# Rows 4 and 5 of a 2-D transform taken from rows 2 and 1, turned in DRAM

## The chip, the cores and the metric

The kernel runs on one core of one Trainium2 chip. The metric is device time in microseconds (us); each kernel is run several times, next to runs of the kernel before on the same chip. Engines: TensorE (PE in the profile; its sequencer PEq), VectorE (DVE), ScalarE (ACT; its DMA queue ACTq), GpSimd (POOL), SyncE (SP; its DMA queue SPq). A profiled run gives a page of summaries and a trace. The record calls a run slow when it is over 1.5% above the fastest of its kernel, and fast otherwise; where slow runs are among those quoted, I say so. "Granted clock" is the share of its full clock that TensorE was given.

## The reference

Four batches, eight heads, 768 tokens of 64 channels. Attention with a band of 96 and 8 global tokens, then a real 2-D Fourier transform over 768 tokens and 512 channels, a normalisation, and a feed-forward product of 512 x 2048 x 512.

```python
def _moe_ref(x, w_ch1, w_ch2) -> np.ndarray:           # x: (4, 768, 512), out of the attention
    X = np.fft.fft(x, axis=1)
    X = np.fft.fft(X, axis=2)
    mixed = np.real(X).astype(np.float32)
    u = x + mixed
    mu = np.mean(u, axis=-1, keepdims=True)
    var = np.mean((u - mu) ** 2, axis=-1, keepdims=True)
    un = (u - mu) / np.sqrt(var + 1e-06)
    ch = np.maximum(un @ w_ch1, 0.0) @ w_ch2
    return (u + ch).astype(np.float32)
```

## The kernel before

Tokens of a batch are handled as six "rows": row r holds the tokens 6m + r, m on the 128 partitions. The attention output x goes to DRAM (`xd`) and comes back in that form (`xr`). The transform over tokens gives y (matmuls `py`), the one over channels gives u (matmuls `pu`, 16 for two rows). Two rows make a chunk, and a chunk goes through normalise, transpose (`ptu` to `unT`, from batch 2 on by DMA), `ph` and `pg`, the two feed-forward products. A y with its columns backwards, kept for a second use, is a mirror copy. A static plan in Python orders the work of each engine once, at build time.

Other names in the lines below: `qs` and `vs` are loaded q, k and v, `pt` the transposes of q and k (into `qkT`), `sc` the attention scores, `er` their exponentials, `zy` a y copied out of PSUM, `hT` a `ph` copied out, `ob` a finished row. A fill matmul is one whose result nobody uses. PSUM is the memory in which the results of matmuls lie; the kernel uses it in pieces called banks.

```python
PAIRS = ((1, 2), (0, 3), (4, 5))                       # rows of the three chunks of a batch
...
def rd():                                              # x comes back by rows
    XR[b] = buf("xr", b, [P, NS, Dm], FP16, 3)
    for c in ((0, 3), (3, 6)):
        eng.dma_start(XR[b][:, c[0]:c[1]], XD[b].rearrange("(m r) d -> m r d", r=6)[:, c[0]:c[1]])
...
def ysrc(rs, rd):                                      # where a y comes from: direct, or a mirrored copy
    if (rs, rd) in POS:
        return rs, rd, False
    return (6 - rs) % 6, (4 - rd) % 4, True
...
# u_unit: one pu group of 16 matmuls for each of the three chunks
for (a, rd), (r2, d2, mir) in src.items():
    yy = Y[(b, r2, d2, "r") if mir else (b, r2, d2)]
    o = pu[:, a, rd * P:(rd + 1) * P]
    for x in range(2):
        nc.tensor.matmul(o, yy[:, x, :], t2_sb[:, rd, (0 if x == 0 else (2 if mir else 1)), :],
                         start=(x == 0), stop=(x == 1))
...
# the result of a row goes out in one DMA
(nc.scalar if c < 6 else nc.sync).dma_start(out[b].rearrange("(m r) d -> m r d", r=6)[:, rs, :], cell[0])
```

The softmax here doesn't subtract the row's maximum and nothing guards it: scores larger than these inputs give would overflow.

## Time and profile before

| | before |
|---|---|
| time, median of 3 | 272.46 us (272.37 to 273.26) |
| profiled span | 270.1 us, granted TensorE clock 1.000 |
| real matmul work in 10 us (columns / 2400, fill left out), 50 to 260 us | 8.7 to 10.1 us |
| DMA moved | 41.25 MB |

The page gives busy time by engine and the chain of work that ended last. The lines that carry the reading stand in the prediction below.

### The profile page before, as it was taken

What the parts mean: (1) busy time and instruction counts of PE and PEld (TensorE: products, weight loads), DVE (VectorE), ACT (ScalarE), POOL (GpSimd) and SP (SyncE); (2) the same over time, 40 slices, a digit from 0 to 9 for tenths busy, and PEclk for the clock granted to TensorE, in tenths of its full rate; (3) what the DMA queues carried; (4) which work ended last, traced back from release to release, by engine and by line L of the source; (5) the groups of instructions that cost most, each with busy time, mean ns of one, the idle gap of its engine ahead of it and who ended that gap; (6) DMA issues with size and microseconds to landing.
All of it is one profiled execution on the core that took longest, in us unless ns stands there. A gap on an engine that the chain in (4) does not pass through costs nothing.

```text
span 270.1 us, 6015 instructions
## 1 busy us (share of the span) xinstructions
PE 257.7 (95%) x2425; PEld 174.3 (65%) x2425; DVE 177.0 (66%) x357; ACT 136.9 (51%) x234; POOL 72.5 (27%) x125
## 2 busy tenths in 40 slices
PE   7789899999999999999999999999989999999994
PEld 3345587787775456767887655687676666767443
DVE  4576938767699999975799777789964424211112
ACT  2877437778631327868344557882464252515000
POOL 1582708549214572363001320120000010100000
PEclk9999999999999999999999999999999999999999
DMA  7999979999999998998059982024602221210122
GB/s 209 292 274 311 205 228 213 206 200 205 201 231 293 287 271 209 219 174 137 0 149 245 143 197 61 0 43 110 203 0 44 95 62 55 62 41 38 40 80 78
DMA packets 82447, 41.25 MB, mean 153 GB/s; under 512 B 45812, under 2 KB 78068, under 8 KB 82292
## 3 DMA queue, kind: packets, MB, share of 16 engines
q1 hardware_dynamic: 70804, 28.81, 48.8%
q0 software_dynamic: 4224, 4.19, 9.7%
q10 hardware_dynamic: 7392, 7.87, 9.7%
q8 instruction: 19, 0.31, 0.5%
q14 instruction: 8, 0.07, 0.1%
HBM read 32.47 MB, written 9.44 MB: 155 GB/s over the span
## 4 chain that ended last, share of the span: by engine, by line
PE 79%; DVE 11%; SPq 3%; DMA 2%; issue 1%; POOL 1%; ACT 1%; DVEq 0%; POOLq 0%
PE ph L1103 32%; PE pg L1126 24%; PE pu L990 4%; PE sc L569 4%; PE pav L698 3%; DVE x L718 2%; PE pt L531 2%; DMA qs<-in_q_dram 2%; PE py L901 2%; SPq L405 2%; PE pg L1155 1%; PE py L905 1%; PE ptu L1072 1%; PE pav L687 1%; PE py L908 1%
## 5 line engine op out<-in xcount | busy, mean ns | idle before, releaser
L1103 PE MATMUL ph<-unT,w 128*128 128x256 f16 x768 | 94.9, 273 | 0.0
L1126 PE MATMUL pg<-w,hT 128*128 128x512 f16 x368 | 86.0, 379 | 0.0
L1103 PEld LDWEIGHTS <-w 128*128 128x128 f16 x768 | 71.8, 98 | 15.9 <-issue 4.4
L1109 ACT ACTIVATE hT<-ph 128x512 f16<-128x512 f32 x59 | 35.1, 597 | 54.0 <-PE ph L1103 52.2
L1126 PEld LDWEIGHTS <-hT 128*128 128x128 f16 x368 | 35.1, 98 | 35.7 <-issue 1.1
L592 ACT ACTIVATE er<-sc 128x992 f16<-128x992 f32 (+2 forms) x42 | 38.0, 924 | 19.6 <-DMA qs<-in_q_dram 7.2
L1137 DVE SCALAR_TENSOR_TENSOR ob<-pg,sm,u 128x512 f32<-128x512 f32 x23 | 17.2, 748 | 44.4 <-PE pg L1126 33.8
L1110 DVE TENSOR_SCALAR hT<-ph 128x512 f16<-128x512 f32 x37 | 25.4, 688 | 14.4 <-PE ph L1103 14.1
L423 POOL CAST qk<-qs 128x768 f16<-128x768 f32 x25 | 22.6, 908 | 44.7 <-DMA qkT<-qk 18.8
L607 DVE TENSOR_TENSOR ex<-er,mk 128x992 f16<-128x992 f16 (+2 forms) x42 | 27.6, 672 | 3.5 <-ACT er L592 3.4
L1047 POOL TENSOR_SCALAR sm<-sm 128x2 f32<-128x2 f32 x12 | 2.8, 233 | 74.6 <-ACT un L1040 74.2
L1011 DVE SCALAR_TENSOR_TENSOR u<-pu,xr 128x512 f32<-128x512 f32 x24 | 15.7, 686 | 6.3 <-PE pu L990 6.2
L718 DVE TENSOR_TENSOR x<-pav,rc 128x512 f16<-128x512 f32 (+1 forms) x27 | 17.1, 632 | 1.2 <-DVE rc L717 0.3
L569 PE MATMUL sc<-qkT 64*128 64x256 f16 (+1 forms) x192 | 16.4, 261 | 0.6 <-ACT v L470 0.4
L1040 ACT ACTIVATE un<-un 128x512 f16<-128x512 f16 x24 | 14.9, 622 | 3.3 <-DMA unT<-un 2.9
L698 PEld LDWEIGHTS <-ex 128*128 128x128 f16 x352 | 15.0, 97 | 2.0 <-DVE rc L717 0.4
L698 PE MATMUL pav<-v,ex 128*128 128x65 f16 x352 | 16.1, 193 | 0.0
L922 ACT ACTIVATE zy<-py 128x512 f16<-128x512 f32 x16 | 9.2, 593 | 12.8 <-DVE eA L855 8.0
L569 PEld LDWEIGHTS <-qkT 64*128 64x128 f16 x192 | 6.3, 94 | 12.0 <-issue 9.3
L479 POOL CAST v<-vs 128x768 f16<-128x768 f32 x12 | 11.8, 980 | 7.6 <-DMA vs<-in_v_dram 7.5
L330 PE MATMUL fill<-eg 128*128 128x512 f16 x45 | 12.4, 424 | 1.4 <-DVE eg L1188 1.2
L540 DVE COPY qkT<-pt 128x1536 f16<-128x1536 f16 x12 | 11.4, 952 | 1.1 <-PE pt L531 1.0
(109 smaller groups left out, 288.5 us busy)
## 6 DMA issues: line engine op xcount, KB each, us to landing
vs<-in_v_dram SPq DMA_DIRECT2D x24, 192.0 KB, 6.9
w<-in_moe_w_ch_dram POOLq DMA_DIRECT2D x8, 512.0 KB, 9.7
qs<-in_q_dram SPq DMA_DIRECT2D x9, 384.0 KB, 6.8
qs<-in_k_dram SPq DMA_DIRECT2D x9, 384.0 KB, 7.3
out_dram<-ob ACTq DMA_DIRECT2D x12, 256.0 KB, 3.4
out_dram<-ob SPq DMA_DIRECT2D x11, 256.0 KB, 2.0
xd<-x ACTq DMA_DIRECT2D x12, 192.0 KB, 3.3
xr<-xd ACTq DMA_DIRECT2D x6, 384.0 KB, 3.9
```

Of the source, the lines that this page charges most:

```text
L423: nc.gpsimd.tensor_copy(d, s)
L569: nc.tensor.matmul(pa[:, s, c0:c0 + cw], TT[n][lo:lo + 64, 1, i * P:(i + 1) * P], TT[n][lo:lo + 64, 0, i * P:i * P + cw], start=(not inps) ...
L592: A(mine(), cut(pa), AF.Exp, 0.0, 0.125)
L607: VT(o, mine(), m, op=ALU.mult)
L698: nc.tensor.matmul(po[:, jj, hh * 65:(hh + 1) * 65], lhsT, v16[b % 2][:, i, h, 0:65], start=(jp == 0 and a == 0), stop=(a == len(ops) - 1) ...
L718: VT(X[b][:, 2 * jp:2 * jp + 2, first * Dh:(first + nh) * Dh].rearrange("p j (h d) -> p j h d", d=Dh), pv[:, :, :, 0:Dh], rc.to_broadcast( ...
L1011: V.scalar_tensor_tensor(u[:, a].rearrange("p (n r) -> p n r", r=4), pu[:, a].rearrange("p (r n) -> p n r", r=4), 1.0, XR[b][:, (r0, r1)[a ...
L1103: nc.tensor.matmul(ph[:, a * CH:(a + 1) * CH], w1[:, d, jb * P:(jb + 1) * P], UNT[c][:, d, :], start=(d == 0), stop=(d == ND - 1))
L1109: pl.later([("ACT", act(512), lambda: A(dst, ph, AF.Relu)), ("DVE", dve(512), lambda: V.tensor_scalar_max(dst, ph, 0.0))], [], e, [("h", c ...
L1110: ("DVE", dve(512), lambda: V.tensor_scalar_max(dst, ph, 0.0))],
L1126: nc.tensor.matmul(pg, HT[c][:, jb, t * P:(t + 1) * P], w2[:, jb, :], start=(jb == 0), stop=(jb == NJ - 1))
L1137: V.scalar_tensor_tensor(cell[0], pg, MV[c][:, t, 3:4], UT[c][:, t, :], op0=ALU.mult, op1=ALU.add)
```

## The change

The transform of a real x has a symmetry: row 6 - r is row r with columns and tokens backwards. So rows 5 and 4 need no `pu` of their own, if x is added in turned form and the result is turned back. Columns can be read backwards on chip; tokens lie on partitions and are turned in DRAM, x once (`xe`) and each result row once (`oe`). A second part is for batch 0: three tokens are summed on VectorE first, so that 16 `py` matmuls vanish, and the first chunk is put ahead of later work.

```diff
+            rows = XD[b].rearrange("(m r) d -> m r d", r=6)
 ...
+            XE[0] = dr.tile([2, P, Dm], FP16, tag="xe", name=f"xe_{b}", bufs=2)
+            eng.dma_start(XR[b][0], rows[:, 1:3])
+            eng.dma_start(XE[0], rows[::-1, 4:6].rearrange("m a d -> a m d"))      # turned in DRAM
+            eng.dma_start(XR[b][2], rows[:, 0:4:3])
 ...
+        pl.later([(on, 0.5, lambda: eng.dma_start(XR[b][1][:, :, 0:Dm], XE[0].rearrange("a p d -> p a d")))], [("xr", b)], 0.0,
 ...
-    PAIRS = ((1, 2), (0, 3), (4, 5))
+    PAIRS = ((1, 2), (5, 4), (0, 3))
 ...
+                if pr == 1:                                     # u of rows 5 and 4 from the pu of rows 1 and 2
+                    o, xx = u[:, a, 1:Dm + 1], xr[:, 1 - a, 1:Dm + 1]
+                    i = pu[:, a].rearrange("p (r n) -> p r n", r=4)[:, ::-1, ::-1].rearrange("p r n -> p n r")
 ...
+        def g3():                                               # batch 0: sums of three before py, on VectorE
 ...
+            def back():                                         # second hop of a turned result
+                o = out[b].rearrange("(m r) d -> m r d", r=6)[::-1, rs, :]
+                eng.dma_start(o.rearrange("m (h d) -> h m d", h=2), cell[1].rearrange("m (h d) -> h m d", h=2))
```

(Cut: the mirror copies that go, edge columns, the order of units, four casts, those of two head pairs, moved to ScalarE, constants of the plan.)

## The prediction

> **What bounds the kernel now.** I read the page first, then the chain of waits in order of time, then the timeline by engine around the places where that chain changes owner. From the page, the engine shares, the chain's shares and the two costliest groups:
>
> ```profile
> PE 257.7 (95%) x2425; PEld 174.3 (65%) x2425; DVE 177.0 (66%) x357; ACT 136.9 (51%) x234; POOL 72.5 (27%) x125
> ...
> PE 79%; DVE 11%; SPq 3%; DMA 2%; issue 1%; POOL 1%; ACT 1%; DVEq 0%; POOLq 0%
> ...
> L1103 PE MATMUL ph<-unT,w 128*128 128x256 f16 x768 | 94.9, 273 | 0.0
> L1126 PE MATMUL pg<-w,hT 128*128 128x512 f16 x368 | 86.0, 379 | 0.0
> ```
>
> TensorE carries 79% of the chain that ends last, two thirds of it in the two feed-forward products (ph and pg). Busy 95% is not proof of full use, so I counted columns: matmul columns divided by 2400 per us. From 0 to 46 us real work fills about two thirds of the time (the rest is waiting and fill matmuls); from 50 us to 260 us every stretch of 10 us holds 9.1 to 10.5 us of it. So there are two regimes: a start limited by a chain of dependences, and after 46 us a TensorE that is simply full. The chain of waits shows the border:
>
> ```profile
> 34.07 5.44 PE py L901 x48
> 39.51 0.89 PE pu L990 x16
> ...
> 45.17 0.89 PE pu L990 x16
> 46.06 0.87 PE ph L1103 x8
> ...
> 49.01 0.87 PE ph L1103 x8
> ```
>
> 48 py matmuls take 5.44 us (0.113 each), 16 pu matmuls 0.89 us, and the first ph starts at 46.06 us. After that TensorE idles visibly only three times, 1.66 us in all. The timeline (start, duration; in brackets idle before it and what ended it):
>
> ```profile
> 85.28 0.29 PE L687 MATMUL pav<-vG,eg 128*128 128x260 f16 x1 [0.26 <-DVE x L718]
> 103.27 0.27 PE L905 MATMUL py<-t,eA 128*128 128x256 f16 x1 [0.50 <-DVE zy L924]
> 201.18 1.05 PE L990 MATMUL pu<-t,zy 128*128 128x128 f16 x16 [0.90 <-ACT zy L922]
> ```
>
> The DMA queue of SyncE matters for what follows. Its issues, and the GpSimd cast that waits for the last of them:
>
> ```profile
> 34.84 0.81 SPq L745 DMA_DIRECT2D xr<-xd  x2
> ...
> 42.50 2.81 SPq L371 DMA_DIRECT2D vs<-in_v_dram  x2
> 45.42 2.94 SPq L405 DMA_DIRECT2D qs<-in_k_dram  x1
> 53.98 0.83 POOL L423 CAST qk<-qs 128x768 f16<-128x768 f32 x1 [0.27 <-DMA qs<-in_k_dram]
> ```
>
> A load issued at 45.42 us landed at 53.95 us: 8.5 us later. By the landing times in the trace the vs loads ahead of it (issued from 42.50) landed at 51.4 and 52.3 us. The queue is backlogged all the way from 36 to 54 us.
>
> **What the Trainium skill says.** (1) "DMA: Bandwidth & Descriptors", section Queues, rings and completion order: SyncE owns one ring on each of 16 DMA engines, and each consumes descriptors in ring order. The trace agrees: landings from this queue come in the order of issue, 1 to 2 us apart, at 42.5, 44.1, 44.9, 45.6, 50.1, 51.4, 52.3, 53.9 us. (2) Same page, Latency and other measured facts: two of the engines are usually slower. The trace agrees that the last engine sets a landing: the load landing at 42.5 us had half of its engines done by 40.2. (3) "TensorE: Matmul & The Clock Gate", section Back-to-back issue gap: N/2.4 + 2.5 ns warm, which is 56 and 109 ns for 128 and 256 columns; the trace has 0.89/16 = 55.6 ns and 0.113 us. (4) "Perfetto Trace Analysis", Sequencer Loop: an instruction waits for its semaphore in its engine's queue. Each engine's order is fixed when the kernel is built, so one late operand holds everything behind it.
>
> **The change part by part.**
> - Rows 4 and 5 of the transform reuse the product of rows 2 and 1: four groups of 16 pu matmuls vanish, 4 x 0.89 = 3.56 us of TensorE. In batch 0, rows 0 and 3 are summed on VectorE first: 16 of 60 py matmuls vanish, 16 x 0.113 = 1.81 us. The built order confirms both: 2425 matmuls become 2346 (one more is a fill). **Sum 5.4 us**, nearly all on the full engine.
> - 16 mirror copies vanish (12 on ScalarE 7.1 us, 2 on VectorE 0.6, 2 on GpSimd 1.2). Beside other work, but they end the 0.90 us idle at 201 us.
> - Added on VectorE: six sums in batch 0 (before the py evictions; 2 x 0.42 + 4 x 0.28 = 2.0 us by the rows of equal shape) and edge-column copies (8 x 0.17 = 1.3 us over the kernel). Both hidden, in my judgement: the py in front of them runs to 38.2 us, and the sums should end near 37.4.
> - Added on DMA: per batch 256 KB turned in DRAM and read back, and two stores turned through DRAM. Late in the kernel the DMA share is low (0.14 to 0.4 in the rows by stretch after 160 us), so nothing there; the last chunk is not turned.
> - First chunk's chain: with 8 fewer py before it pu starts about 0.6 us earlier (then limited by the y evictions), ends near 39.75; add, normalise, transpose, copy follow without the mirror copies on ScalarE and without pu 2 and 3 on TensorE. 39.75 + 0.95 (add of a row with its sum, to the end of sm) + ScalarE free at 41.3, normalise 0.65, transpose 0.3, two copies of 0.42 and waits: the first ph near **43.3 instead of 46.06**.
>
> If that were all: 5.4 us of work less, about 0.6 us more idle at the start, up to 1.7 us of gaps gone: 272.5 - 5.4 + 0.6 - 1 = about 266.7.
>
> **The new wait.** The built order shows what stands behind it. VectorE: two copies of the first chunk's transpose, then a copy of an edge column of the turned tokens (xr1), add of rows 5 and 4, and only then the eviction of the first and second ph. ScalarE: normalise of that second chunk before it evicts the third ph. TensorE: ph, ph, one qk transpose, then a third ph that waits for VectorE's first eviction, since ph has two buffers. On SyncE the read of xr1 is issued after both vs loads of the second head pair, exactly the slot before the 45.42 issue. By ring order it lands after 52.3 us; with 256 KB where the next load had 384 KB (landed 53.9), I estimate **53.2 us**. Then VectorE needs 0.15 (column) + 1.5 (two adds, timed at 0.69 + 0.08 each) + 0.35 (column, mean) + 0.7 (eviction) = 2.7: third ph near 55.9. TensorE was out of work at 43.3 + 1.75 + 0.8 = 45.9. **A stall of 10 us.**
>
> The sum, from the third ph on: before, 270.1 - 49.0 = 221.1 us remained. After, add ptu 0.45 and pu 0.89 not done yet, take 3 x 0.89 for batches 1 to 3: 219.8; less about 1 us of gaps: 218.8. End 55.9 + 218.8 = 274.7 us of span; timed runs are 2.0 to 2.4 us above the span, so about **276.8**, and I say 276.5 because the chain of batch 1 gets its data ready during the stall.
>
> **The rivals.**
> 1. xr1 lands early, because fewer descriptors stand ahead than I think or the queue drains faster: the stall shrinks to 0 to 4 us and the time is 266.5 to 271. For: its issue needs only the turned rows, in DRAM by about 40 us, and 46 us would be enough. Against: landing order equals issue order in every case I looked at.
> 2. The stall is there but is repaid: batch 1 loses its later waits on VectorE, 97% busy from 80 to 110 us. At most the 1.66 us of gaps plus the start of batch 1: 273 to 276.
> 3. Worse: ScalarE now casts two head pairs of batch 2, issues the turned reads, and waits for each store to land before turning it (3.4 us to landing in the row of stores from ScalarE). It is 51% busy, but waits in order delay the exponentials; 1 to 3 us more: 278 to 280.
> 4. TensorE work does not matter at all, hidden behind VectorE: against it, real work of 10 us in nearly every 10 us after 50.
>
> **Range and chances.** I give the long stall 75 to 80%, centred at 276.5 with about 2 us either way; a small one or none the rest, spread from 266 to 272. The limits at 2% are 267.0 and 277.9. Faster needs no stall and all the saved work: 0.08. Slower needs the stall and rival 3 or a landing past 54 us: 0.24. The rest 0.68.
>
> **What would show each step.** The page: pu 128 instead of 192 matmuls, py 116 instead of 132, TensorE busy lower although matmuls wait. First ph at 43 to 44 us. In the list of waits, VectorE at the edge-column copy waits for the DMA of xr1, and TensorE's third ph (or its idle before) waits on VectorE; TensorE empty from 46 to 56 us. xr1 landing at 52 to 54.5 us. The gap at 201 us gone; span from third ph to the end 218 to 221 us. The prediction is wrong if xr1 lands before 48 us, if VectorE's order lets ph evictions pass, or if the freed 5.4 us comes back as idle after 80 us.

## The result

| | before | after |
|---|---|---|
| time, median | 272.86 us (one more run than above) | 316.85 us (315.67 to 319.12, 4 runs) |
| profiled span | 270.1 us | 316.1 us |
| mean granted clock | 1.000 | 0.932 |
| matmuls | 2425 | 2346 |
| DMA moved | 41.25 MB | 44.38 MB |

The ratio is 1.162 (95% interval 1.154 to 1.170): slower, and far outside the predicted range. Ratios here are the mean time of one kernel's fast runs over that of the other's of the same rounds, so not quite the ratio of the medians quoted. Outputs were correct, here and in all experiments.

From the page of the kernel after: busy time, two rows of the span in 40 equal slices (7.9 us each, in tenths), and the chain of waits by engine.

```profile
PE 264.3 (84%) x2346; PEld 174.4 (55%) x2346; DVE 176.3 (56%) x369; ACT 134.6 (43%) x226; POOL 65.5 (21%) x119
...
PE   8888961899999862789999589989999999999930
...
PEclk9999995599999967799999969999999999999995
...
PE 41%; DMA 24%; DVE 11%; SPq 8%; issue 6%; POOL 5%; ACT 2%; ACTq 1%; POOLq 0%; DVEq 0%
```

TensorE's share of the chain fell from 79 to 41%, DMA's rose from 2 to 24%. There are several holes: near 50 us, near 115 and 125 us, near 180 us and at the end. Fewer matmuls show *more* busy time (264.3 against 257.7 us), because the clock row drops to 5 to 7 at the holes. In real work by columns the stretches 50 to 60 us, 110 to 120 and 120 to 130 hold a share of 0.17, 0.33 and 0.17; before, these were all about 1.0.

The first hole is the predicted one. TensorE's timeline (start, duration, instruction, idle before it and what ended it), then the chain:

```profile
43.19 1.91 PE L1129 MATMUL ph<-unT,w 128*128 128x256 f16 x16 [0.17 <-DVE unT L1110]
...
56.80 3.57 PE L1129 MATMUL ph<-unT,w 128*128 128x256 f16 x16 [6.42 <-DVE hT L1136]
```

```profile
49.51 4.83 DMA xr<-xe
...
54.36 0.18 DVE xr L1021
```

The first `ph` starts at 43.19 us, the turned tokens land at 54.34 us, VectorE touches them at 54.36, and the third `ph` starts at 56.80 us. From there to the end of the span are 259.3 us, where the prediction had 218.8: **the 40 us by which the time exceeds the prediction (316.85 against 276.5) all lie after the stall that was foreseen**.

The next hole, near 110 to 127 us. ScalarE, its DMA queue and SyncE's in the timeline:

```profile
109.30 3.20 ACTq L751 DMA_DIRECT2D xr<-xd  x1
112.61 1.00 ACT L592 ACTIVATE er<-sc 128x992 f16<-128x992 f32 x1 [7.43 <-DMA qs<-in_k_dram]
...
126.40 0.60 ACT L945 ACTIVATE zy<-py 128x512 f16<-128x512 f32 x1 [11.45 <-DMA vs<-in_v_dram]
```

```profile
118.37 0.25 SPq L1289 DMA_DIRECT2D hold<-xr  x1
...
120.10 5.27 SPq L371 DMA_DIRECT2D vs<-in_v_dram  x4
```

VectorE writes the row that the store behind it takes, and ScalarE sends that store (both in the kernel after); then two lines of the kernel before, for comparison, its reads of x on ScalarE and 12 transposes:

```profile
110.25 0.74 DVE L1163 SCALAR_TENSOR_TENSOR ob<-pg,sm,u 128x512 f32<-128x512 f32 x1
...
126.03 0.32 ACTq L1172 DMA_DIRECT2D oe<-ob  x1
```

```profile
94.38 0.88 ACTq L745 DMA_DIRECT2D xr<-xd  x2
...
114.03 0.84 PE L531 MATMUL pt<-ident,qk 128*128 128x128 f16 x12
```

TensorE in the kernel after:

```profile
113.66 1.44 PE L531 MATMUL pt<-ident,qk 128*128 128x128 f16 x12 [4.46 <-ACT er L592]
...
127.05 0.37 PE L928 MATMUL py<-t,eA 128*128 128x256 f16 x1 [6.76 <-ACT zy L945]
```

ScalarE needs 3.20 us to get one DMA issued behind the turn (L751; the first issue of the same group took 0.33 us), and computes nothing for 7.43 us: 2.5 us of it until x is in DRAM (107.64 us), then 4.8 us for three issues. Later it stands for 11.45 us until a load of another queue has landed. In its way is the store `oe<-ob`, whose row was ready at 110.99 us. The trace's semaphore records show why it waits for that load: the landings of both are told on the same semaphore, and the store went out right after the load's last signal there, at 125.95 us. (No run gives the store a semaphore of its own.) That load was held back too: SyncE may send batch 3's loads only when `xr` of batch 1 has landed (`hold`, at 118.37 us), and that landing stood behind the turn. TensorE waits 4.46 and 6.76 us, and after the wait 12 transposes take 1.44 us, where the kernel before takes 0.84 us in the same view.

And the end of the kernel: the last pieces of the chain, and the DMA engines from 297 to 304 us in 40 slices of 0.175 us (mean share of 16 engines in tenths, then GB/s).

```profile
296.76 7.09 DMA oe<-ob
...
304.57 7.83 DMA out_dram<-ob
...
312.51 0.48 DVE ob L1201
```

```profile
DMA  0111037898111111111111111111111111111000
GB/s 23 53 47 47 35 76 304 351 404 304 47 53 47 47 47 47 53 47 47 53 47 47 47 47 53 47 47 53 47 47 47 53 47 53 59 47 47 0 0 0
```

This is the clearest view of the cause. For 5 us only one tenth of the engines' time is used, at 47 GB/s: one turn of 256 KB. 256 KB at 47 GB/s are 5.6 us. The packets tell the same: 256 of 1024 bytes at a mean of 46 ns, some 46 to 48 of them per us, so about 46 x 0.047 = 2.1 in flight. **Two of the sixteen engines carry the whole turn.** The semaphore records say so directly: a turn in 16 blocks, in the first experiment below, signals its landing 16 times, each turn of this kernel only 3 times, once about 1.1 us after the issue and twice at its end (303.19 and 303.21 us for this one). From issue to landing these turns took 7.8 to 11.3 us. The straight store of 256 KB issued behind this turn, at 296.76 us, ran at 304 to 404 GB/s (slices 7 to 10), but it is complete only when its parts behind the turn are through: `oe<-ob` needed 7.09 us from issue to landing.

The Trainium skill has the rule, which the prediction missed ("DMA: Bandwidth & Descriptors", section Why a DMA increments its semaphore by 16 and not by 1): the number of engines is the largest number up to 16 that divides the slowest dimension of size other than 1 of both access patterns. The turn is written with `a` = 2 outermost, so two engines; the trace agrees with 2.1 packets in flight and two late signals. The same turn with a dimension of 16 outermost should use all, which is the first experiment.

### The profile page after: what moved, and what is told of

It is laid out like the page before. It is cut to its first block, busy times and chain, and to the rows that moved or that the text cites. A ratio compares the mean times of both kernels' runs of the same rounds, so it can differ in the third digit from the quotient of the medians.

```text
span 316.1 us, 5868 instructions
## 1 busy us (share of the span) xinstructions
PE 264.3 (84%) x2346; PEld 174.4 (55%) x2346; DVE 176.3 (56%) x369; ACT 134.6 (43%) x226; POOL 65.5 (21%) x119
## 2 busy tenths in 40 slices
DMA packets 87142, 44.38 MB, mean 140 GB/s; under 512 B 45900, under 2 KB 83276, under 8 KB 86988
## 3 DMA queue, kind: packets, MB, share of 16 engines
q10 hardware_dynamic: 10398, 9.70, 10.5%
## 4 chain that ended last, share of the span: by engine, by line
PE 41%; DMA 24%; DVE 11%; SPq 8%; issue 6%; POOL 5%; ACT 2%; ACTq 1%; POOLq 0%; DVEq 0%
PE ph L1129 16%; PE pg L1152 14%; DMA xe<-xd 6%; DMA oe<-ob 5%; SPq L371 4%; SPq L405 3%; DMA vs<-in_v_dram 3%; DVE x L718 3%; DMA w<-in_moe_w_ch_dram 3%; DMA out_dram<-ob 2%; DMA qs<-in_q_dram 2%; PE sc L569 2%; PE pu L998 2%; DVE u L1030 2%; POOL qk L423 2%
## 5 line engine op out<-in xcount | busy, mean ns | idle before, releaser
L1129 PE MATMUL ph<-unT,w 128*128 128x256 f16 x768 | 96.4, 276 | 7.5 <-DVE hT L1136 7.2
L1152 PE MATMUL pg<-w,hT 128*128 128x512 f16 x368 | 88.2, 386 | 0.0
L1129 PEld LDWEIGHTS <-w 128*128 128x128 f16 x768 | 72.8, 99 | 25.8 <-issue 13.8
L1135 ACT ACTIVATE hT<-ph 128x512 f16<-128x512 f32 x62 | 36.8, 597 | 55.0 <-PE ph L1129 46.7
L1136 DVE TENSOR_SCALAR hT<-ph 128x512 f16<-128x512 f32 x34 | 23.3, 688 | 18.3 <-PE ph L1129 17.9
L423 POOL CAST qk<-qs 128x768 f16<-128x768 f32 x21 | 18.1, 873 | 15.0 <-DMA qs<-in_q_dram 5.7
L512 POOL COPY kG<-qkT 64x8 f16<-64x8 f16 x32 | 9.2, 287 | 53.5 <-DVE qkT L540 27.4
L531 PE MATMUL pt<-ident,qk 128*128 128x128 f16 x144 | 12.4, 245 | 8.9 <-ACT er L592 4.5
L1052 ACT ACTIVATE un<-u,sm 128x512 f16<-128x512 f32 x12 | 8.4, 718 | 20.0 <-DVE sm L1035 19.9
L947 DVE CAST zy<-py 128x512 f16<-128x512 f32 x11 | 7.4, 688 | 15.9 <-ACT zy L945 9.7
```

The source lines that it names most:

```text
L423: nc.gpsimd.tensor_copy(d, s)
L1129: nc.tensor.matmul(ph[:, a * CH:(a + 1) * CH], w1[:, d, jb * P:(jb + 1) * P], UNT[c][:, d, :], start=(d == 0), stop=(d == ND - 1))
L1135: pl.later([("ACT", act(512), lambda: A(dst, ph, AF.Relu)), ("DVE", dve(512), lambda: V.tensor_scalar_max(dst, ph, 0.0))], [], e, [("h", c ...
L1136: ("DVE", dve(512), lambda: V.tensor_scalar_max(dst, ph, 0.0))],
L1152: nc.tensor.matmul(pg, HT[c][:, jb, t * P:(t + 1) * P], w2[:, jb, :], start=(jb == 0), stop=(jb == NJ - 1))
```

## The experiments

The theory after the result: turning on two engines makes landings late, and everything that is behind a turn, in rings or in the order of an engine, waits. The main rivals: it is the added traffic itself, or the work moved to ScalarE. (The four casts moved there stay in the runs up to `e6` and were not tested by themselves.)

### Sixteen column blocks instead of two

The same bytes turned, in the same place of every queue.

```diff
-            eng.dma_start(XE[0], rows[::-1, 4:6].rearrange("m a d -> a m d"))
+            eng.dma_start(XE[0].rearrange("m (x d) -> x m d", x=16),
+                          XD[b].rearrange("(m r) d -> m (r d)", r=6)[::-1, 4 * Dm:6 * Dm].rearrange("m (x d) -> x m d", x=16))
 ...
-                eng.dma_start(o.rearrange("m (h d) -> h m d", h=2), cell[1].rearrange("m (h d) -> h m d", h=2))
+                eng.dma_start(o.rearrange("m (h d) -> h m d", h=16), cell[1].rearrange("m (h d) -> h m d", h=16))
```

> The changed kernel with one edit: all turns through DRAM (of the tokens and of the stores) are cut into 16 column blocks with the block as outermost dimension, instead of 2; instruction orders on all engines are the same. Theory A (a turn cut in 2 runs on only 2 DMA engines, takes 5 to 8 us and holds up what is behind it): the turns land in 2 to 3 us, the stalls of TensorE after 100 us and at the tail go, about 276 us remain (the stall at 46 to 56 us that I predicted stays). Theory B (the second hop through DRAM with its waits in the issuing engine's order is what costs, on however many engines): above 300 us.

Measured: 291.25 us, ratio 1.066 (1.064 to 1.068): 25.6 of the 44 us are gone with the shape of an access pattern. The turns now land 3.6 to 7.1 us after their issue. Both numbers expected were missed, theory A's 276 us by 15, theory B's "above 300" by 9. The clock rises from 0.932 to 0.970. The end of its chain:

```profile
278.36 2.92 DMA oe<-ob
...
281.94 3.63 DMA out_dram<-ob
```

The two waits of 7.09 and 7.83 us are now 2.92 and 3.63 us. The stall at the start stays: its third `ph` waits 8.89 us, until 55.27 us.

Each half alone, tokens first:

> Only the token turns (4) are cut in 16, the 8 turned stores stay on 2 blocks. Theory A: the stalls that begin at the token turns (about 110 to 127, 178 to 183, 236 us) shrink, those of the stores stay (the wait of 8 us before the last add and about 3 us near 205 us): 288 to 298 us. Theory B: as the changed kernel, 310 to 320 us.

Measured: 307.86 us, ratio 1.125 (1.119 to 1.131), 9.0 us less than after: between the two theories, 288 to 298 and 310 to 320.

And the stores alone:

> Only the 8 turned stores are cut in 16, the token turns stay on 2 blocks. Theory A: the tail is 10 to 12 us shorter, the stalls behind the token turns stay in part: 292 to 304 us. Theory B: 310 to 320 us.

Measured: fast runs 297.32 and 299.15 us, two more slow (302.11 and 303.38), ratio 1.091 (1.086 to 1.096), as theory A had it. In points of the ratio the tokens are worth 3.7, the stores 7.1, both together 9.6 and not 10.8; the difference is about as large as the intervals allow by chance. So the effects nearly add, and the stores were the larger part.

### The turned tokens of batch 0 read early

The kernel with all turns in 16 blocks, with one DMA moved in SyncE's order: the read of batch 0's turned tokens ahead of the first load of v instead of behind the second.

```diff
-        ... [("xr", b)], 0.0,
-                 [("xrb", b)], lat=2.0, dma=0.7)
+        ... [("xr", b) if b else ("xe0", 0)], 0.0,
+                 [("xrb", b)], lat=2.0, dma=0.7, rank=1 if b else 0)
```

> As the first run of this call, and in batch 0 the read of the turned tokens (xr1) is issued before the first v load of batch 1 instead of after the second; no other engine's order changes. Theory of the slot (the read lands late only because it stands behind two v loads and a q load in its queue): it lands near 44 to 45 us instead of 54, TensorE's stall of about 10 us from 46 us falls to 1 to 2 us, the whole is 8 to 9 us shorter than the first run, about 267 us. Rival (the read lands late because turning takes that long): no change.

Measured: 281.98 us, ratio 1.033 (1.025 to 1.040), 9.3 us less: the difference is as expected, though not the total, which built on the 276 us missed above. The read goes out at 39.55 and lands at 45.76 us. TensorE's third `ph`, then what is left near 100 us (ScalarE, TensorE):

```profile
48.22 3.31 PE L1129 MATMUL ph<-unT,w 128*128 128x256 f16 x16 [2.44 <-DVE hT L1136]
```

```profile
99.98 4.25 ACTq L751 DMA_DIRECT2D xr<-xd  x1
104.33 1.00 ACT L592 ACTIVATE er<-sc 128x992 f16<-128x992 f32 x1 [8.35 <-DMA xe<-xd]
```

```profile
105.38 1.44 PE L531 MATMUL pt<-ident,qk 128*128 128x128 f16 x12 [5.44 <-ACT er L592]
```

So the predicted stall was real and worth 9.3 us. The next wait is again ScalarE, held 4.25 us by one issue behind a turn, now a spread one: it is the crowded queue and not only the two engines.

### Whose queue waits

The same, with all reads and turns of x issued by SyncE instead of ScalarE (for batch 0 they were there already).

```diff
-        on, eng = ("ACT", nc.scalar) if b else ("SP", nc.sync)
+        won, weng = ("ACT", nc.scalar) if b else ("SP", nc.sync)     # the writes of x stay
+        on, eng = "SP", nc.sync
```

> The fourth run (all turns in 16 blocks, xr1 of batch 0 early) with one edit: the three reads of the tokens and the read of the turned tokens are issued on SyncE for every batch, not on ScalarE for batches 1 to 3. Theory D (ScalarE stands still at 96 to 104 us because these issues are ahead of its exponentials in its order and wait for the write of the tokens to land; 5.4 us of TensorE idle and the slow clock after it follow): the stall at 100 to 105 us goes, 5 to 9 us less than the fourth run, 273 to 277 us. Rival (VectorE is what is late there, or the loads): no change, 281 to 283 us.

Measured: ratio 1.023 (1.017 to 1.029), and the wait of 5.44 us is 2.33 us. The four runs took 275.46, 277.54, 280.35 and 280.86 us; the last two are slow, but the ratio takes them in. The two fast ones lie near theory D's 273 to 277 us, while the run before took 280.63 to 284.68 us, all fast; but the intervals of the two ratios overlap. So a gain is likely, and its size, 3 to 6 us, is open.

Then the second hop of every store on SyncE as well:

```diff
-                pl.later([("ACT" if c < 6 else "SP", 0.45, back)], ...)
+                pl.later([("SP", 0.45, back)], ...)
```

> As the run before, and the second hop of every turned store is issued on SyncE, so ScalarE never waits for the first hop to land. Theory D: another 1 to 4 us less, 270 to 275 us. Rival: no change against the run before; if SyncE's own order (loads behind waits for stores) now matters, 2 to 5 us more.

Measured: 283.86 us, ratio 1.037 (1.031 to 1.043), not better: the rival's case. The waits that left ScalarE came back on SyncE, in front of the transposes that it issues for the scores of batch 3. TensorE in the timeline ("issue": nothing that the profile shows was waited for; the chain before it runs through SyncE's queue and `xr<-xe`):

```profile
164.39 0.60 PE L569 MATMUL sc<-qkT 64*128 64x256 f16 x4 [8.12 <-issue]
```

### A turn that nobody reads

The kernel before, with one unused turn of rows 4 and 5 per batch, behind the reads of x. No `pu` is saved, no store is turned. This measures the turn by itself.

```diff
+            xe = dr.tile([2, P, Dm], FP16, tag="xe", name=f"xe_{b}", bufs=2)
+            eng.dma_start(xe, XD[b].rearrange("(m r) d -> m r d", r=6)[::-1, 4:6].rearrange("m a d -> a m d"))
```

> The kernel before with one unused copy per batch added behind the reads of the tokens: rows 4 and 5, tokens backwards, DRAM to DRAM, in 2 blocks as in the changed kernel; nothing reads it. Theory A: 256 KB take 5 to 6 us of two DMA engines' time and hold up what is queued behind them on those two: 1 to 8 us more than before (274 to 281), mostly where loads of batch 1 are late. Rival (a turn as such is cheap, only the chain of waits costs): within 1 us of before.

Measured: 287.1 us, ratio 1.051 (1.049 to 1.054): 1 MB of unused copies cost 14 us, more than even theory A had (1 to 8).

> The same added copy in 16 blocks. Theory A: all 16 engines share it, it lands within 2 to 4 us, the time is within 2 us of before and below the run with 2 blocks. Rival: as the run with 2 blocks, or worse since its packets are of 128 bytes (2048 instead of 256 per turn).

Measured with 16 blocks: 278.24 us, ratio 1.017 (1.011 to 1.024): the same bytes on all engines cost 5 us, where theory A had at most 2. Both parts are real: a smaller one for the copy as such, a larger one for the two engines. The 5 us are those of this form, in packets of 128 bytes instead of 1024; a copy on all engines in larger packets was not run.

Where does it cost? The two-block turn in batches 0 and 1 only, then in 2 and 3 only:

> The same unused turn of two blocks in batches 0 and 1 only, whose reads of x fall at 43 and 90 to 110 us, where the loads and the weights fill the DMA engines. Theory: nearly all of the 14 us that the four cost, 11 to 15 us, ratio 1.040 to 1.055, with stalls of TensorE at 50, 101 and 113 us as with four. Rival: half, some 7 us.

> The kernel before with an unused turn of two blocks (rows 4 and 5, the form of the change) behind the reads of x, in batches 2 and 3 only, where the DMA engines are mostly idle. All four cost 14 us. Theory (the cost is set by what is queued behind a turn on its two engines, and late only output stores and weight-free work are): at most 2 us, ratio 1.000 to 1.008. Rival (the cost is one of the turn itself, whatever else is on the queues): half of it, some 7 us, ratio 1.02 to 1.03.

Measured: early 286.13 us, ratio 1.046 (1.041 to 1.051); late 272.70 to 274.95 us (a fourth run, 277.50, is slow), ratio 1.001 (0.996 to 1.006). TensorE's list of waits (us in total, times, longest) of the early one from 40 to 120 us:

```profile
PE py L908 <- ACT zy L925: 7.4, 1, 7.4
PE pt L531 <- POOL qk L423: 2.8, 2, 2.1
```

The late one from 140 us on:

```profile
PE ph L1106 <- DMA unT<-un: 0.9, 1, 0.9
```

The same slow copy costs nothing that can be measured where nobody needs what stands behind it, and nearly all of the 14 us where the loads of the next batches do.

### Batch 0's part alone

The sums of batch 0 in the kernel before, nothing turned, then with the guard that keeps VectorE from the second `pu` group until the first chunk's `unT` is copied.

```diff
+        def g3():                                   # as in the change
 ...
+        if b == 0:
+            pl.later([("DVE", 2.0, g3)], [("w", b, 1)], 0.0, [("w", b, 2)])
 ...
-                    if (b, g, t) == (0, 2, 0):
+                    if (b, g, t) == (0, 1, 1):
                         u_unit(b, 0)
```

> The kernel before with the one part of the change that turns nothing: batch 0's sums of three tokens on VectorE, so that its 60 py matmuls become 44, and the first pu group ahead of the third group of py. Nothing is added on any DMA queue. Theory (the whole loss of the change came from the turns through DRAM and their place in the queues; this part was sound): first ph near 43.5 to 44.5 us instead of 46.1, 16 py of 0.113 us = 1.8 us less on TensorE, time 269.5 to 272.5, ratio 0.985 to 0.998. Rival (the 2 us more of VectorE work in batch 0 holds up the copies that the next pu groups wait for, or the early TensorE work was not the bound there): first ph early but a gap of 1 to 3 us before the third ph, ratio 1.00 to 1.01.

Measured: 276.45 us, ratio 1.013 (1.008 to 1.017). The first `ph` begins at 46.27 us, no earlier than before, and new waits of TensorE follow: 2.85 us (`sc` for the copy of `qkT`) up to 98.91 us, 0.74 and 0.77 us near 113, and 1.41 us up to 156.86. (The next expectation puts the last one at 114 us by mistake.)

```diff
-                         [("xr", b)] + free("u", HP + c) + ...
+                         [("xr", b)] + free("u", HP + c) + ([("unT", 0)] if c == 1 else []) + ...
```

> The sums of batch 0 without turns once more (273.7 us profiled, ratio 1.0126), now with the second half of that part of the change: VectorE adds x to the second pu group only when the first chunk's unT is copied. In the run without it VectorE spent 41.86 to 44.6 us on two u groups before the copy of unT at 45.29, and the first ph began at 46.27, no earlier than before. Theory (the guard is what makes the first ph early): first ph at 43.5 to 44.5 us; if nothing is lost later, 269.5 to 272.5 us, ratio 0.985 to 0.998. Rival (the later batches lose what is won, as with the sums alone, which had waits of 2.9 us at sc near 96 and 1.4 us at pu near 114 that before has not; a new order of VectorE and ScalarE work in batch 1): first ph early, but ratio 1.000 to 1.015.

Measured: 279.88 us, ratio 1.024 (1.020 to 1.028); the first `ph` at 47.05 us. My theory of this part fell in both runs. The guard was also not the whole one: the change holds back its second and third chunk (`c in (1, 2)`), this run only the second, and the third went in front. Here the transposes of the first chunk begin only at 43.96 us, just after VectorE is through with the third `pu` group at 43.85; I take it that they waited for that group's PSUM bank, which no run tests. In the change no such group is in front. It lost again later:

```profile
72.53 0.51 PE L531 MATMUL pt<-ident,qk 128*128 128x128 f16 x6 [3.79 <-POOL qk L423]
```

That cast waited for a load of k, 12.87 us under way (the kernel before has a median of 7.9 us for loads of k from 30 to 75 us). Why that one took longer stays open. What follows is modest: this part is no gain by itself, as built here, and with its full guard it was not tried.

### Turned rows only where the DMA engines are idle

The kernel before for batches 0 and 1, the change's rows 5 and 4 for batches 2 and 3 (or 3 alone), turns in 16 blocks and issued by SyncE.

```diff
+    TB = 2                                          # first turned batch; 3 in the second run
-    PAIRS = ((1, 2), (0, 3), (4, 5))
+    PAIRS = [((1, 2), (0, 3), (4, 5)) if b < TB else ((1, 2), (5, 4), (0, 3)) for b in range(B)]
+        pl.later([("SP", 0.45, turn)], [("xri", b)], 0.0, [("xe", b)], lat=2.0, dma=0.7)
+        pl.later([("SP", 0.45, lambda: nc.sync.dma_start(XT[b][:, :, 0:Dm], ...))],
+                 [("xe", b), ("xr", b)], 0.0, [("xrb", b)], lat=2.0, dma=0.7)
```

> The kernel before for batches 0 and 1, and the turned rows of the change for batches 2 and 3 only, each turn in 16 column blocks, all turns issued by SyncE (which has nothing but transposes and stores there). It saves two of the four pu groups, 2 x 0.89 = 1.8 us of TensorE work, and the mirror copies of those batches; an unused turn in these two batches cost nothing (ratio 1.0009). Theory (the saving of TensorE work is real where TensorE never waits, and the loss of the change lay with the early batches): 270.5 to 273 us, ratio 0.988 to 0.999. Rival (somebody has to wait for the turned rows, and the waits of the change at 183 and 236 us, 4.9 and 2.7 us, come with the scheme itself): ratio 1.005 to 1.03, with waits of TensorE between 160 and 240 us on the turned rows.

> The same with batch 3 alone turned: one pu group less, 0.9 us of TensorE work. Theory: ratio 0.993 to 1.001. Rival: half the loss of the run with two batches, or nothing if its waits are all in batch 2.

Measured: two batches 280.43 us, ratio 1.027 (1.023 to 1.032); batch 3 alone 271.93 us, ratio 0.996 (0.993 to 0.998). The six runs of the first range from 276.53 (the profiled one) to 282.13 us, two of them slow, and the ratio takes those in; slower it is by either count. The second is the first kernel here that is faster than before, clear of noise: 1.2 us (0.4 to 2.0) for one `pu` group of 0.89 us and its mirror copies. Batch 2's loss shows as one long wait (SyncE's queue, then TensorE):

```profile
153.47 0.59 SPq L764 DMA_DIRECT2D xe<-xd  x1
157.51 0.58 SPq L766 DMA_DIRECT2D xr<-xe  x1
```

```profile
162.41 0.58 PE L572 MATMUL sc<-qkT 64*128 64x240 f16 x4 [5.12 <-DVE u L1056]
```

x was in DRAM at 142.9 us, but SyncE was still at loads and transposes, some of which waited (for TensorE, for casts on GpSimd), and sent the turn at 153.47 us. So only the place in the order was changed next. First the turn, from SyncE to ScalarE's queue, right behind the reads of x:

```diff
             eng.dma_start(XR[b], rows[:, 0:4])
+            if b == 2:
+                turn(eng)
```

(Cut: what the plan is told about it; the read of the turned rows also gets a new place in its list of needs.)

> Batches 2 and 3 turned as in the run that was 2.7% slower, with one change: batch 2's turn is issued by ScalarE right behind its reads of x (some 141 us) instead of by SyncE, where it stood behind a transpose that waited for a cast on POOL and went out at 153.47 us; the reading of the turned rows stays on SyncE. Theory (the 5.1 us that sc waited for the second pu group's bank come from that place in SyncE's order, not from turning rows): the read goes out near 153.5 instead of 157.5, lands near 156.7, the wait falls to about 1 us, ratio 0.990 to 1.004. Rival (turned rows of batch 2 cost by themselves, by the traffic or by the added work of VectorE): 1.015 to 1.03 again.

Measured: 275.88 us, ratio 1.012 (1.006 to 1.017). The theory's sign was right and its size wrong: the wait fell from 5.12 to 4.05 us, not to 1, because the *read* of the turned rows still stood behind transposes, which took longer here:

```profile
156.60 0.58 SPq L770 DMA_DIRECT2D xr<-xe  x1
```

```profile
161.64 0.58 PE L572 MATMUL sc<-qkT 64*128 64x240 f16 x4 [4.05 <-DVE u L1060]
```

Then that read ahead of the last two pairs of transposes:

```diff
-            pl.later([("SP", 1.2, xbar)], [("qk", n, 0), ("qk", n, 1)] + free("qkT", n), ...
+            pl.later([("SP", 1.2, xbar)], [("qk", n, 0), ("qk", n, 1)] + ([("xrq", 2)] if hp > 1 else []) + free("qkT", n), ...
```

> The last run with one instruction moved: SyncE reads batch 2's turned rows at some 148 us, ahead of the last two pairs of transposes of qk, instead of at 156.60 us behind them (they waited for a cast on POOL, and that for a load). The turn itself is issued at 141 us and should have landed. Theory (batch 2's loss is one of place in SyncE's order): the read lands near 151.5, before its pu group is through at 156.3, the wait of 4.0 us at sc is gone, ratio 0.988 to 0.998. Rival (turning batch 2's rows costs by itself, or the load that its traffic delays holds up the casts and so the scores of batch 3): ratio 1.003 to 1.02, with a wait of sc or pt near 155 to 165 us.

Measured: **270.94 us, ratio 0.993 (0.988 to 0.997)**, the fastest kernel, profiled span 268.0 us; its other five spans are 268.5 to 270.8, those of the kernel before in the same rounds 270.1 to 272.8 us. The interval lies below 1.

```profile
150.96 0.56 SPq L770 DMA_DIRECT2D xr<-xe  x1
```

```profile
158.02 0.38 PE L572 MATMUL sc<-qkT 64*128 64x240 f16 x4
```

The same `sc` now starts at 158.02 us with no idle in front of it. In batches 2 and 3 the saving agrees with what the prediction counted: 2 x 0.89 = 1.8 us of `pu`; 2.0 us measured (0.7 to 3.2), with the mirror copies gone too.

## Why the prediction was wrong

- **TensorE work saved, 5.4 us.** Right as a count (2346 matmuls, `pu` 128 instead of 192) and, for the `pu` groups, right in worth where nothing waits, within the intervals: one group gained 1.2 us, two gained 2.0. The 1.81 us of `py` in batch 0 were never seen as a gain. In the change as given it was drowned.
- **First `ph` near 43.3 us.** 43.19 us. **The new wait**: landing at 53.2 us predicted, 54.34 measured; third `ph` 55.9 predicted, 56.80 measured; "A stall of 10 us" was worth 9.3 us when it was taken away. **The gap at 201 us** is gone. These steps held, and for the reason given: the two vs loads in front landed at 52.71 and 53.79 us, in the order of issue.
- **The step that failed** is the line on DMA: "per batch 256 KB turned in DRAM and read back, and two stores turned through DRAM. Late in the kernel the DMA share is low [...] so nothing there; the last chunk is not turned." It counted bytes against a mean share of 16 engines. In its place the runs showed: a turn that keeps two engines for 5.6 us and lands 7.8 to 11.3 us after its issue (25.6 us of the loss went with 16 blocks), delays of whatever is behind it, and 5 us for the unused copies even when spread. The end of the kernel contradicted "nothing there" by itself: the last chunk is not turned, but its output buffers and its stores wait behind the turned rows of the chunk before, 7.09 and 7.83 us. One half of the step was right: an unused turn in batches 2 and 3 cost nothing that can be measured. It is the waiting for it, and the early batches, that cost.
- **Rival 3, ScalarE waits in order, "1 to 3 us more".** That ScalarE's waits in order cost was right; what it waits for and the size were not. In batch 1 alone it stood still 7.43 us (4.8 of it issuing) and 11.45 us (a semaphore shared with a late load), and TensorE 4.46 and 6.76 us with it; in batch 2 it stood 5.52 us until the turn of x had landed (182.15 us). The wait that the rival named, a store's first hop, shows once, with 2.90 us at 206.50 us. "Slower" had been given 0.24 for this rival or a landing past 54 us; the landing came at 54.34 us, but that is not what made the change slower.
- **A term that was not there**: TensorE's clock. After a long wait matmuls run slower (12 transposes in 1.44 us, not 0.84; 16 `ph` in 3.57 us, not 1.91), and the mean grant was 0.932. Of the same matmuls, 264.3 us were busy in the change and 258.9 us with turns in 16 blocks, 5.4 us apart. The Trainium skill has this too ("TensorE: Matmul & The Clock Gate", section Part 1: The HAM clock gate): idle for about a window halves the clock until work has lasted again, which agrees with the nearly doubled durations in the trace.
- **Small slips of the prediction**, without effect on its result. Real work in 10 us, counted anew, is 8.7 to 10.1 us, not 9.1 to 10.5, and from 0 to 46 us it fills little over half the time, not two thirds. The landings said to be 1 to 2 us apart are 0.7 to 4.5 us apart. The turned rows were in DRAM at 42.73 us, not "about 40". And the load landing at 42.5 us had not half but 15 of its 16 engines done by 40.4 us: one late engine alone sets the landing, by 1.2 to 2.3 us in the four loads behind it too.

Of the 16.2 points of the ratio, 9.6 went with 16 blocks, 3.3 with the early read, about 1.0 with the reads on SyncE (not resolved; 2 by its fast runs), and 2.3 are left. Four unused spread turns cost 1.7 by themselves, so the rest is likely traffic in the full stretch from 35 to 110 us, against a saving of 2.0 (5.4 us); that is argued, not shown, and the parts of that remainder, the four casts on ScalarE among them, were not separated.

## What to carry to other kernels

Before a DMA is called free because the engines are mostly idle, ask how many engines its access pattern uses and who stands behind it, in its rings, in the order of the engine that issues it, and at the buffers it frees. Put a dimension that 16 divides outermost, also when copying from DRAM to DRAM. A saving on a full engine is real, but it is kept only when each new operand is issued, and landed, before its user: moving one DMA instruction was worth 9.3 us in one place, and moving two turned a loss of 2.7% into a gain of 0.7% in another.

## What the Trainium skill lacked or had wrong

- "DMA: Bandwidth & Descriptors": no measured rate for a DRAM-to-DRAM copy that uses two engines. Here 256 KB in 1024-byte packets ran at 47 GB/s, 46 ns a packet, 5.6 us, and landed 7.8 to 11.3 us after the issue. Its rule for the number of engines agreed (about 2.1 packets in flight, two signals at the end).
- The same page: nothing on how long an engine is held in issuing a DMA while earlier ones are queued. Here one issue took 3.20 and 4.25 us on ScalarE, where the first of the same group took 0.33 us, and in the kernel before the issue of a v load on SyncE took 0.59 to 3.33 us.
- The same page tells to wait on the first copy's semaphore before a dependent one, but not what that costs when the same engine also computes: ScalarE stood still 5.52 us for a turn and 2.90 us for a store's first hop.
- No page gives what it costs when DMAs of two queues share a completion semaphore: a store whose row was ready at 110.99 us went out at 126.03 us, after a load of the other queue, and ScalarE stood 11.45 us.
- No page gives what a copy that nobody reads costs the rest of a kernel: 1 MB in four turns on two engines cost 14 us, on sixteen 5 us, and half of it in idle stretches nothing (ratio 1.001).
